# Sinkhorn attention in front of an expert layer: k and v mixed on the chip, straight into the layouts that attention reads

## The chip, the cores and the metric

The kernel runs on one core of one Trainium2 chip. The metric is the device time of one execution in microseconds (us), lower is better. A profile of one execution, with a trace of every instruction and transfer, is there for each kernel. The executions compared here were all in the fast state, apart from two small measuring kernels with a single run each, whose state is unknown. Some of them came from other chips of the same kind, on which the kernel before took 717 to 719 us instead of 710, so kernels from different chips are compared by their ratio to the kernel before, timed in the same rounds on the same chip.

Engine names in the profile: PE is TensorE (PEld its weight loads), DVE is VectorE, ACT is ScalarE, POOL is GpSimd, SP is SyncE, which here only issues transfers.

## The reference

Attention with sorted blocks, then a layer with eight experts. The change concerns the first part alone.

```python
B, H, S, D = 4, 8, 768, 64          # 32 heads; 8 blocks of 96 rows each
P = sort_net                        # [4, 8, 8, 8]
for _ in range(5):                  # Sinkhorn
    P = exp(P - P.max(-1)); P = P / P.sum(-1); P = P / P.sum(-2)
k_sorted = einsum('bhij,bhjcd->bhicd', P, k_b)   # block i is a mix of 8 blocks
v_sorted = einsum('bhij,bhjcd->bhicd', P, v_b)
attn = softmax(q_b @ k_sorted^T / sqrt(D))       # inside each block of 96 rows
x = attn @ v_sorted                 # to [3072, 512], row = (batch, position)
# then: router picks one of 8 experts a row (argmax of x @ w_gate + bias);
# out[row] = gate * relu(x[row] @ w1[e]) @ w2[e]
```

## The kernel before

P is normalised on VectorE, written to memory and read back as block-diagonal 128x128 matrices `bd`, with 32 small loads. Sixteen heads at a time, one matmul mixes 512 columns of k or v; the result goes to scratch memory. Attention then reads q, mixed k and mixed v head by head in runs of one 64-element row.

```python
for g in range(2):
    # ... bd: 16 loads of 8x8 blocks of P from memory ...
    for which, src_v, dst_v in ((0, k_bh, ks_v), (1, v_bh, vs_v)):
        rhs = sb.tile([128, BLK * D], BF16)          # ... loaded ...
        for c in range(12):
            acc = psum.tile([128, 512], FP32)
            nc.tensor.matmul(acc, bd, rhs[:, c * 512:(c + 1) * 512], start=True, stop=True)
            res = sb3.tile([128, 512], BF16)
            nc.scalar.copy(res, acc)                 # dense eviction
            nc.gpsimd.dma_start(out=dst_v[...][:, c * 512:(c + 1) * 512], in_=res)
# ...
for bh in range(BH):
    if bh % 4 == 1: load_weights(bh // 4)            # two loads of 1 MB
    # ... loads of q, mixed k, mixed v of this head, 128-byte runs ...
    for g in range(2):
        # 8 transposes of q and k into tp; copy qkT <- tp on VectorE
        # 4 matmuls sc_p = q k^T; exponential on ScalarE
        # row sums and reciprocal on VectorE
        # 4 transposes of attn into atp; copy attnT <- atp on VectorE
        # 4 matmuls o_p = attnT v
        # 4 scalings by the reciprocal, half on VectorE, half on ScalarE
    # after 8 heads: x rows stored
```

The router, the prefix sums, the scatters of row numbers and the expert loop follow; they are the same in both kernels.

The softmax here doesn't subtract the row's maximum and nothing guards it: scores larger than these inputs give would overflow.

Of the kernel before, what the change touches and what calls it, by code (L numbers as in the profile page):

```python
# [9 lines left out]
FP32 = mybir.dt.float32  # L10
# [7 lines left out]
def kernel(  # L18
# [23 lines left out]
    P_dram = nc.dram_tensor("P_scratch", [BH, NB, NB], FP32, kind="Internal").ap()  # L42
    ks_dram = nc.dram_tensor("ks_scratch", [BH, NB, BLK, D], BF16, kind="Internal").ap()
    vs_dram = nc.dram_tensor("vs_scratch", [BH, NB, BLK, D], BF16, kind="Internal").ap()
# [9 lines left out]
    singles = ctx.enter_context(tc.tile_pool(name="singles", bufs=1))  # L54
    ph1 = ExitStack()
    sb = ph1.enter_context(tc.tile_pool(name="sb", bufs=2))
    sb3 = ph1.enter_context(tc.tile_pool(name="sb3", bufs=3))
    psum = ph1.enter_context(tc.psum_pool(name="psum", bufs=2))
    psum2 = ph1.enter_context(tc.psum_pool(name="psum2", bufs=2))

    ident = singles.tile([128, 128], BF16)
    make_identity(nc, ident)

    P_t = singles.tile([BH, NB, NB], FP32)
    nc.gpsimd.dma_start(out=P_t, in_=sort_net.rearrange("b h i j -> (b h) i j"))
    red = singles.tile([BH, NB], FP32)
    for it in range(5):
        nc.vector.tensor_reduce(red, P_t, AX.X, ALU.max)
        nc.vector.tensor_tensor(P_t, P_t, red.broadcast_to([BH, NB, NB]), ALU.subtract)
        nc.scalar.activation(P_t, P_t, ACT.Exp)  # L70
        nc.vector.tensor_reduce(red, P_t, AX.X, ALU.add)
        nc.vector.reciprocal(red, red)
        nc.vector.tensor_tensor(P_t, P_t, red.broadcast_to([BH, NB, NB]), ALU.mult)
        P_swap = bass.AP(tensor=P_t.tensor, offset=P_t.offset,
                         ap=[P_t.ap[0], P_t.ap[2], P_t.ap[1]])
        nc.vector.tensor_reduce(red, P_swap, AX.X, ALU.add)
        nc.vector.reciprocal(red, red)
        colb = bass.AP(tensor=red.tensor, offset=red.offset,
                       ap=[red.ap[0], [0, NB], red.ap[1]])
        nc.vector.tensor_tensor(P_t, P_t, colb, ALU.mult)  # L80
    nc.gpsimd.dma_start(out=P_dram, in_=P_t)

    k_bh = k.rearrange("b h (n c) d -> (b h) n (c d)", n=NB)
    v_bh = v.rearrange("b h (n c) d -> (b h) n (c d)", n=NB)
    ks_v = ks_dram.rearrange("g n c d -> g n (c d)")
    vs_v = vs_dram.rearrange("g n c d -> g n (c d)")

    for g in range(2):
        bd = sb.tile([128, 128], BF16)
        nc.vector.memset(bd, 0.0)  # L90
        for l in range(16):
            bh = g * 16 + l
            src = bass.AP(tensor=P_dram.tensor, offset=P_dram.offset + bh * 64,
                          ap=[[1, NB], [NB, NB]])
            nc.gpsimd.dma_start(out=bd[l * 8:(l + 1) * 8, l * 8:(l + 1) * 8], in_=src)  # L95
        for which, src_v, dst_v in ((0, k_bh, ks_v), (1, v_bh, vs_v)):
            rhs = sb.tile([128, BLK * D], BF16)
            nc.gpsimd.dma_start(
                out=rhs.rearrange("p (a f) -> p a f", a=16),
                in_=src_v[g * 16:(g + 1) * 16].rearrange("g n f -> (g n) f")  # L100
                    .rearrange("p (a f) -> p a f", a=16))
            for c in range(12):
                acc = psum.tile([128, 512], FP32)
                nc.tensor.matmul(acc, bd, rhs[:, c * 512:(c + 1) * 512],  # L104
                                 start=True, stop=True)
                res = sb3.tile([128, 512], BF16)
                nc.scalar.copy(res, acc)  # L107
                nc.gpsimd.dma_start(  # L108
                    out=dst_v[g * 16:(g + 1) * 16]
                        .rearrange("g n f -> (g n) f")[:, c * 512:(c + 1) * 512],  # L110
                    in_=res)

    ph1.close()
    I32 = mybir.dt.int32
    from concourse.masks import make_upper_triangular
    wpool = ctx.enter_context(tc.tile_pool(name="wpool", bufs=1))
    w1_all = wpool.tile([128, E, 4 * F], BF16, tag="w1_all")
    w2_all = wpool.tile([128, E, 8 * Dm], BF16, tag="w2_all")
# [35 lines left out]
    scale = 1.0 / (D ** 0.5)  # L154
    ph2 = ExitStack()
    apool = ph2.enter_context(tc.tile_pool(name="apool", bufs=3))
    apsum = ph2.enter_context(tc.psum_pool(name="apsum", bufs=2))
    for bh in range(BH):
        b, h = bh // H, bh % H
        if bh % 4 == 1:  # L160
            load_weights(bh // 4)
        if h == 0:
            xacc = [apool.tile([BLK, 4, H, D], BF16, tag=f"xacc{gg}",
                               name=f"xacc{gg}")
                    for gg in range(2)]
        qks = apool.tile([BLK, NB, 2, D], BF16)
        nc.gpsimd.dma_start(out=qks[:, :, 0],  # L167
                            in_=q[b, h].rearrange("(n r) d -> r n d", r=BLK))
        nc.scalar.dma_start(out=qks[:, :, 1],
                            in_=ks_dram[bh].rearrange("n r d -> r n d"))  # L170
        vs_all = apool.tile([BLK, NB, D], BF16)
        nc.sync.dma_start(out=vs_all,
                            in_=vs_dram[bh].rearrange("n r d -> r n d"))
        for g in range(2):
            tp = apsum.tile([D, 8 * BLK], BF16, tag="tp")
            for j in range(4):
                nc.tensor.transpose(tp[:, j * BLK:(j + 1) * BLK],  # L177
                                    qks[:, 4 * g + j, 0], ident[:BLK, :BLK])
                nc.tensor.transpose(tp[:, (4 + j) * BLK:(5 + j) * BLK],  # L179
                                    qks[:, 4 * g + j, 1], ident[:BLK, :BLK])  # L180
            qkT = apool.tile([D, 8 * BLK], BF16, tag="qkT")
            nc.vector.tensor_copy(qkT, tp)  # L182
            sc_p = apsum.tile([BLK, 4 * BLK], FP32, tag="sc")
            for j in range(4):
                nc.tensor.matmul(sc_p[:, j * BLK:(j + 1) * BLK],  # L185
                                 qkT[:, j * BLK:(j + 1) * BLK],
                                 qkT[:, (4 + j) * BLK:(5 + j) * BLK],
                                 start=True, stop=True)
            attn = apool.tile([BLK, 4, BLK], BF16, tag="attn")
            nc.scalar.activation(attn.rearrange("p a f -> p (a f)"), sc_p,  # L190
                                 ACT.Exp, scale=scale)
            rs = apool.tile([BLK, 2, 4], FP32, tag="rs")
            nc.vector.tensor_reduce(rs[:, 0], attn, AX.X, ALU.add)  # L193
            nc.vector.reciprocal(rs[:, 1], rs[:, 0])
            atp = apsum.tile([BLK, 4 * BLK], BF16, tag="atp")
            for j in range(4):
                nc.tensor.transpose(atp[:, j * BLK:(j + 1) * BLK],  # L197
                                    attn[:, j], ident[:BLK, :BLK])
            attnT = apool.tile([BLK, 4 * BLK], BF16, tag="attnT")
            nc.vector.tensor_copy(attnT, atp)  # L200
            o_p = apsum.tile([BLK, 4 * D], FP32, tag="op")
            for j in range(4):
                nc.tensor.matmul(o_p[:, j * D:(j + 1) * D],  # L203
                                 attnT[:, j * BLK:(j + 1) * BLK],
                                 vs_all[:, 4 * g + j], start=True, stop=True)
            for j in range(4):
                if j % 2 == 0:
                    nc.vector.tensor_scalar(xacc[g][:, j, h],  # L208
                                            o_p[:, j * D:(j + 1) * D],
                                            rs[:, 1, j:j + 1], None, ALU.mult)  # L210
                else:
                    nc.scalar.activation(xacc[g][:, j, h],  # L212
                                         o_p[:, j * D:(j + 1) * D],
                                         ACT.Copy, scale=rs[:, 1, j:j + 1])
        if h == H - 1:
            for gg in range(2):
                dst = bass.AP(
                    tensor=x_dram.tensor,
                    offset=x_dram.offset + (b * S + 4 * gg * BLK) * Dm,
                    ap=[[Dm, BLK], [BLK * Dm, 4], [1, H * D]])  # L220
                nc.sync.dma_start(
                    out=dst, in_=xacc[gg].rearrange("p j h d -> p j (h d)"))
# [203 lines left out]
```

## Time and profile before

The kernel took 710.56 us (median of the 3 runs made before the prediction, 709.73 to 712.48). The lines that bear on the argument are shown in the prediction; this table sums up where they put the time.

| Stage of the kernel before | from, to (us) | what sets it |
|---|---|---|
| Sinkhorn, `bd` | 0 to 31 | small VectorE steps, then the loads of `bd` |
| mix of k and v | 31 to 100 | stores of the mixed blocks |
| attention | 100 to 306 | 32 heads at 5.27 us are 169 us; the other 37 us are lost to q loads behind weights |
| router, prefix sums | 306 to 386 | many small steps |
| scatters of row numbers | 386 to 488 | 24 transfers one after the other |
| experts | 488 to 711 | matmuls, gathers of rows |

The 306 us at which attention ends is the moment when its last store of x is issued; that store landed at 309.4 us.

### The profile page before, as it was taken

The page shows a single profiled execution, that of the slowest core. Times are in us where ns is not written, and L with a number is a line of the kernel's source. Part 1 is how long each engine was busy: PE and PEld are TensorE (multiplying, and loading weights), DVE is VectorE, ACT ScalarE, POOL GpSimd, SP SyncE. Part 2 cuts the span into 40 slices and gives each one's busy share as a digit, 9 for nine tenths or more (in the row PEclk, how much of TensorE's full clock was granted, in tenths as well). Part 3 has the DMA queues.
Part 4 walks back from the last instruction along what each step waited for, and adds up shares of the span by engine and source line. Part 5 has one row for each costly group of instructions (what it writes and reads, how often), then busy time and mean ns, then how long its engine had stood idle before and what let it go on. Part 6 is the DMA issues. An engine that isn't in the chain of part 4 may idle for free.

```text
span 711.1 us, 8406 instructions
## 1 busy us (share of the span) xinstructions
PE 368.2 (52%) x2424; PEld 217.2 (31%) x2442; DVE 248.1 (35%) x936; ACT 190.8 (27%) x611; POOL 188.6 (27%) x263
## 2 busy tenths in 40 slices
PE   0133364388665788845520000001887788777782
PEld 0000033376554676623310000000333333333331
DVE  4000014367454667745540000000334344443431
ACT  1033342134232333435530000000333333232331
POOL 3863352032120111002212222222233232232231
PEclk9999999999999999999999999999999999999998
DMA  8567559999999755133300000000121111221110
GB/s 164 46 141 166 142 120 116 180 195 213 191 197 212 80 85 70 17 101 64 61 0 6 0 1 0 0 0 23 38 68 52 60 65 46 68 67 45 41 24 0
DMA packets 117106, 56.27 MB, mean 79 GB/s; under 512 B 93964, under 2 KB 108373, under 8 KB 116550
## 3 DMA queue, kind: packets, MB, share of 16 engines
q0 software_dynamic: 51456, 43.04, 33.7%
q1 hardware_dynamic: 37062, 6.39, 6.9%
q10 hardware_dynamic: 28544, 6.30, 5.3%
q8 instruction: 21, 0.34, 0.2%
q14 instruction: 23, 0.19, 0.1%
HBM read 66.13 MB, written 17.63 MB: 118 GB/s over the span
## 4 chain that ended last, share of the span: by engine, by line
DMA 36%; PE 27%; issue 18%; POOL 7%; DVE 7%; ACT 3%; POOLq 0%; SPq 0%; ACTq 0%; DVEq 0%
DMA qks<-in_q_dram 12%; DMA sidx_scratch<-rg_all,dest_i_all 11%; PE h_p L373 6%; PE y_p L388 5%; DMA x_t<-x_scratch,idxg 4%; PE sc_p L185 3%; PE tp L177 3%; DMA out_dram<-y_sb,idxg 3%; PE hT_p L384 2%; PE atp L197 2%; PE tp L179 2%; DVE y_sb L392 2%; DMA idxg<-sidx_scratch 2%; POOL bd L95 2%; POOL ks_scratch L108 2%
## 5 line engine op out<-in xcount | busy, mean ns | idle before, releaser
L367 PE MATMUL xT_p<-ident,x_t 128*128 128x128 bf16 x124 | 20.5, 221 | 143.5 <-DMA x_t<-x_scratch,idxg 127.7
L388 PE MATMUL y_p<-w_all,hT 128*128 x237 | 72.9, 377 | 0.8 <-ACT hT L385 0.8
L177 PE MATMUL tp<-ident,qks 96*64 96x96 bf16 x256 | 49.1, 283 | 32.4 <-DMA qks<-in_q_dram 30.6
L182 DVE COPY qkT<-tp 64x768 bf16<-64x768 bf16 x64 | 34.6, 540 | 88.4 <-PE tp L179 88.4
L361 POOL DMA_INDIRECT x_t<-x_scratch,idxg x31 | 30.4, 980 | 129.8 <-PE h_p L373 56.9
L373 PE MATMUL h_p<-w_all,xT 128*128 x241 | 59.0, 386 | 10.1 <-issue 8.6
L104 PE MATMUL acc<-rhs,bd 128*128 128x512 bf16 x48 | 27.2, 586 | 71.2 <-ACT res L107 39.2
L167 POOL DMA_DIRECT2D qks<-in_q_dram x32 | 24.9, 779 | 143.9 <-PE tp L179 139.6
L368 ACT COPY xT<-xT_p 128x128 bf16<-128x128 bf16 x62 | 16.4, 265 | 170.1 <-PE xT_p L367 169.8
L212 ACT ACTIVATE xacc<-o_p,rs 96x64 bf16<-96x64 f32 x128 | 39.3, 307 | 73.6 <-DVE xacc L208 72.5
L367 PEld LDWEIGHTS <-x_t 128*128 128x128 bf16 x124 | 9.5, 97 | 150.0 <-DMA x_t<-x_scratch,idxg 133.5
L384 PE MATMUL hT_p<-ident,h_sb 128*128 128x128 bf16 x248 | 49.5, 220 | 10.2 <-DVE hT L385 9.0
L368 DVE COPY xT<-xT_p 128x128 bf16<-128x128 bf16 x62 | 12.2, 219 | 115.2 <-PE xT_p L367 114.8
L177 PEld LDWEIGHTS <-qks 96*64 96x64 bf16 x256 | 37.3, 159 | 39.6 <-DMA qks<-in_q_dram 32.4
L179 PE MATMUL tp<-ident,qks 96*64 96x96 bf16 x256 | 48.6, 281 | 0.0
L190 ACT ACTIVATE attn<-sc_p 96x384 bf16<-96x384 f32 x64 | 31.1, 486 | 65.0 <-PE sc_p L185 63.9
L185 PE MATMUL sc_p<-qkT 64*96 64x96 bf16 x256 | 42.6, 290 | 7.2 <-DVE qkT L182 7.0
L343 POOL DMA_INDIRECT sidx_scratch<-rg_all,dest_i_all x24 | 23.3, 971 | 79.7 <-DMA sidx_scratch<-rg_all,dest_i_all 75.4
L208 DVE TENSOR_SCALAR xacc<-o_p,rs 96x64 bf16<-96x64 f32 x128 | 35.1, 274 | 25.5 <-PE o_p L203 23.7
L385 DVE COPY hT<-hT_p 128x128 bf16<-128x128 bf16 x124 | 27.9, 225 | 45.5 <-PE hT_p L384 39.4
L107 ACT CAST res<-acc 128x512 bf16<-128x512 f32 x48 | 27.4, 586 | 59.7 <-DMA vs_scratch<-res 26.6
L193 DVE TENSOR_REDUCE rs<-attn 96x4 f32<-96x384 bf16 x64 | 35.0, 547 | 21.7 <-ACT attn L190 21.5
(117 smaller groups left out, 659.2 us busy)
## 6 DMA issues: line engine op xcount, KB each, us to landing
w_all<-in_moe_w_dram POOLq DMA_DIRECT2D x16, 1024.0 KB, 13.3
rhs<-in_k_dram POOLq DMA_DIRECT2D x2, 1536.0 KB, 10.9
rhs<-in_v_dram POOLq DMA_DIRECT2D x2, 1536.0 KB
qks<-in_q_dram POOLq DMA_DIRECT2D x32, 96.0 KB, 16.3
ks_scratch<-res POOLq DMA_DIRECT2D x24, 128.0 KB, 2.1
vs_scratch<-res POOLq DMA_DIRECT2D x24, 128.0 KB, 2.0
qks<-ks_scratch ACTq DMA_DIRECT2D x32, 96.0 KB, 8.7
vs_all<-vs_scratch SPq DMA_DIRECT2D x32, 96.0 KB, 9.6
```

Source lines behind the costliest of these rows:

```text
L177: nc.tensor.transpose(tp[:, j * BLK:(j + 1) * BLK], qks[:, 4 * g + j, 0], ident[:BLK, :BLK])
L179: nc.tensor.transpose(tp[:, (4 + j) * BLK:(5 + j) * BLK], qks[:, 4 * g + j, 1], ident[:BLK, :BLK])
L182: nc.vector.tensor_copy(qkT, tp)
L185: nc.tensor.matmul(sc_p[:, j * BLK:(j + 1) * BLK], qkT[:, j * BLK:(j + 1) * BLK], qkT[:, (4 + j) * BLK:(5 + j) * BLK], start=True, stop=True)
L190: nc.scalar.activation(attn.rearrange("p a f -> p (a f)"), sc_p, ACT.Exp, scale=scale)
L193: nc.vector.tensor_reduce(rs[:, 0], attn, AX.X, ALU.add)
L208: nc.vector.tensor_scalar(xacc[g][:, j, h], o_p[:, j * D:(j + 1) * D], rs[:, 1, j:j + 1], None, ALU.mult)
L212: nc.scalar.activation(xacc[g][:, j, h], o_p[:, j * D:(j + 1) * D], ACT.Copy, scale=rs[:, 1, j:j + 1])
L361: nc.gpsimd.indirect_dma_start(out=x_t, out_offset=None, in_=x_dram, in_offset=bass.IndirectOffsetOnAxis(ap=idx[:, :1], axis=0))
L373: nc.tensor.matmul(h_p, xT[:, c], w1_flat[:, bass.ds(e_sv * (4 * F) + c * F + half * 512, 512)], start=(c == 0), stop=(c == 3))
L384: nc.tensor.transpose(hT_p, h_sb[:, fc * 128:(fc + 1) * 128], ident)
L388: nc.tensor.matmul(y_p, hT[:, fc], w2_flat[:, bass.ds(e_sv * (8 * Dm) + fc * Dm, Dm)], start=(fc == 0), stop=(fc == 7))
```

## The change

The intent is to take the scratch memory for P and for mixed k and v out of the kernel. The matrices `bd` are built on chip. The mix is written with the data as the weights and `bd` as the moving operand, so its result comes out already transposed as the scores want it (k: head dimension on partitions) and as the value matmul wants it (v: block row on partitions). The scores are computed transposed (k rows on partitions), so the exponential writes the operand of the value matmul directly, without transposes; a column of ones beside v gives the row sums. q is loaded in runs of six rows (768 bytes). The core of the diff, with cuts:

```diff
-    for bh in range(BH):
-        ... loads of q, ks, vs; transposes; scores; row sums; transposes; values ...
+    def sort_k(g, ch, act):
+        acc = mipsum.tile([128, 8, 64], FP32, tag="mi", name=f"ka{g}_{ch}")
+        for z in range(8):
+            nc.tensor.matmul(acc[:, z], k_il[:, ch * 8 + z].rearrange("p r d -> p (r d)"), bd_k[g], start=True, stop=True)
+        dst = kTb[g].rearrange("p (x c) -> p c x", c=BLK)[:, ch * 8:(ch + 1) * 8]
+        (nc.scalar.copy if act else nc.vector.tensor_copy)(dst, acc)
+
+    def sort_v(g, ch, act):
+        acc = mipsum.tile([128, 4, 128], FP32, tag="mi", name=f"va{g}_{ch}")
+        for z in range(4):
+            nc.tensor.matmul(acc[:, z], v_cols[:, ch * 4 + z], bd_v[g], start=True, stop=True)
+        dst = v_sb[g].rearrange("p x d -> p d x")[0:BLK, ch * 4:(ch + 1) * 4]
+        (nc.scalar.copy if act else nc.vector.tensor_copy)(dst, acc[0:BLK])
...
+    def expo(u):
+        nc.scalar.activation(attnT[u % 3][...], sc_tiles.pop(u)[0:BLK, :, 0:4 * BLK], ACT.Exp, scale=scale)
...
+    def av(u):
+        if h == 0:
+            x_tiles[g, hf] = apool.tile([BLK, 2, 4, H, D], BF16, tag="xb", bufs=1)
+        for par in range(2):
+            ... 4 matmuls of attnT and v with its column of ones ...
+            nc.vector.reciprocal(rs, op[0:BLK, :, D:D + 1])
+            nc.vector.tensor_tensor(xb[:, par, :, h], op[0:BLK, :, 0:D], rs.broadcast_to([BLK, 4, D]), ALU.mult)
+        if h == 7:
+            for par in range(2):
+                for t in range(6):
+                    nc.sync.dma_start(out=dst, in_=xb[t * 16:(t + 1) * 16, par]...)   # 12 stores of 64 KB
...
+    for e in range(3, E):
+        load_weights(e)          # the space of these held q, k and v until here
```

There are 32 units of attention, each half of the blocks of two heads; 16 units make a group, and the 28 "sort jobs" (12 of k, 16 of v) of group 0 come before the first unit, those of group 1 between the units of group 0.

## The prediction

> **What bounds the kernel now.** I cut the span into stages first, because the page's mean shares (PE 52%, DVE 35%) mix stages with different limits. The chain of waits gives the joints: mixing starts when bd has landed (31 us), the first q transpose stands at 100, the last x store at 306, the last count lands at 368, the scatters of row numbers run from 386 to 488, the expert loop from 488.5 to the end. The view by windows, one row a stage (columns: window, length, then PE, PEld, DVE, ACT, POOL busy us with counts, clock, DMA share, GB/s):
>
> ```profile
> 0.00:20.50 20.50, 0.00 (x0) 0.00 (x0) 8.61 (x42) 2.56 (x6) 5.44 (x13) 1.00 0.90 162
> 20.50:100.00 79.50, 27.22 (x48) 4.97 (x48) 0.00 (x0) 27.32 (x48) 44.48 (x81) 1.00 0.56 125
> 100.00:306.00 206.00, 147.27 (x1280) 117.88 (x1280) 120.67 (x390) 67.35 (x193) 37.77 (x52) 1.00 1.03 138
> 306.00:366.00 60.00, 30.57 (x239) 18.66 (x239) 32.97 (x240) 27.97 (x142) 11.72 (x24) 1.00 0.29 65
> 366.00:386.00 20.00, 0.97 (x7) 0.53 (x7) 3.09 (x16) 1.09 (x7) 4.43 (x9) 1.00 0.04 5
> 386.00:488.50 102.50, 0.00 (x0) 0.00 (x0) 0.00 (x0) 0.00 (x0) 22.99 (x24) 1.00 0.01 0
> 488.50:711.00 222.50, 162.14 (x850) 75.15 (x868) 82.77 (x248) 64.51 (x217) 61.74 (x62) 0.99 0.16 48
> ```
>
> The change works on the first three rows, 306 us; the other 405 us (router, prefix sums, scatters, experts) keep their code. In row two TensorE works 27 of 79.5 us: mixed k and v leave through 48 stores, and the next eviction waits for a store to land. In row three the chain of waits shows two regimes. With the weights in flight:
>
> ```profile
> 111.53 30.32 DMA qks<-in_q_dram
> ...
> 174.26 19.14 DMA qks<-in_q_dram
> 196.50 17.76 DMA qks<-in_q_dram
> 217.37 20.02 DMA qks<-in_q_dram
> ```
>
> Four q loads of 96 KB hold everything for 87 us together; they sit behind 1 MB weight loads on the same queue. Once the weights are in, one head starts every 5.27 us:
>
> ```profile
> 242.22 0.55 PE sc_p L185 x4
> 247.49 0.55 PE sc_p L185 x4
> 252.76 0.55 PE sc_p L185 x4
> ```
>
> So attention is 32 x 5.27 = 169 us by compute, plus about 37 us of load stalls. Which engine sets 5.27 us? From the groups view (mean ns at the end of the busy time):
>
> ```profile
> L182 DVE COPY qkT<-tp 64x768 bf16<-64x768 bf16 x64 | 34.6, 540 | 88.4 <-PE tp L179 88.4
> L193 DVE TENSOR_REDUCE rs<-attn 96x4 f32<-96x384 bf16 x64 | 35.0, 547 | 21.7 <-ACT attn L190 21.5
> L200 DVE COPY attnT<-atp 96x384 bf16<-96x384 bf16 x64 | 22.0, 344 | 34.7 <-PE atp L197 34.4
> L208 DVE TENSOR_SCALAR xacc<-o_p,rs 96x64 bf16<-96x64 f32 x128 | 35.1, 274 | 25.5 <-PE o_p L203 23.7
> L190 ACT ACTIVATE attn<-sc_p 96x384 bf16<-96x384 f32 x64 | 31.1, 486 | 65.0 <-PE sc_p L185 63.9
> L107 ACT CAST res<-acc 128x512 bf16<-128x512 f32 x48 | 27.4, 586 | 59.7 <-DMA vs_scratch<-res 26.6
> ```
>
> Per head VectorE does 2 x (0.540 + 0.547 + 0.164 reciprocal + 0.344) + 4 x 0.274 = 4.3 us. TensorE issues 40 matmuls, which follow each other every 0.08 us in the chain (100.41, 100.49, 100.57 ...), so 3.2 us. Both are near the pace, and the hand-overs between engines make the rest: 5.27 / 4.3 = 1.23, a factor that I use below.
>
> [...] the ks and vs loads are 128 B runs, 96 KB in 8.7 and 9.6 us, while 128 KB of x_t in 1 KB runs takes 2.5 us; 93964 of 117106 packets are under 512 B. [...]
>
> **The change part by part.** Removed: the round trip of P and 32 bd loads (15 to 31 us on the chain), 48 stores and 64 short-run loads of mixed k and v, the transposes of k and of the scores with their copies, the row-sum reductions, and the 128 B runs of q (now 768 B).
>
> (a) Start to mixed group 0. Sinkhorn keeps its pace, 14.5 us less a few (only one max and subtraction). It now shares VectorE with two clearing memsets of k_il (a bd memset of 64 words took 0.112; 3072 words are about 2.8 us each, an estimate) and 12 k copies. The block matrices come from two small matmuls and ten short VectorE steps, some 3 us. Loads: 163 GB/s over the first 18 us, really from 2.4 us on, gives 188 GB/s in bytes written; k, v and two q loads are 1.57 + 1.57 + 0.8 MB, 21 us. k arrives in six pieces through two buffers, and in this trace weight loads run well ahead of the source order (the last of the 16 is issued at 211 us, at about head 18, though the source asks for it at head 29). The weights of experts 0 to 2 depend on nothing now, so one to six of them (5.6 us each at 188 GB/s) will slip in front of late k pieces. I take bd ready at 30 to 35 us. Then 28 sort jobs: 8 or 4 matmuls (0.64 or 0.4 us), an eviction of 512 columns (586 ns ACT, 692 ns for DVE's h_sb), two PSUM buffers: (0.6 + 0.25 + 0.65 + 0.2) / 2 = 0.85 us a job, 24 us. With k late, attention begins at about 60 us.
>
> (b) Attention: 32 units, each as much as one old head. TensorE: 8 + 8 matmuls and 3 transposes, 19 x 0.08 = 1.5 us. [...] VectorE: two reciprocals (0.17) and two products of 256 columns [...], and half a qT copy (0.27): 1.5 us. Times 1.23: 1.9 us, taken as 2.0. Units 0 to 15 carry 28 sort jobs as well: 14 evictions, 12 k copies, q interleaves add some 18 us of VectorE, so (1.5 + 1.1) x 1.23 = 3.2 us a unit. Sum: 16 x 3.2 + 16 x 2.0 = 83 us.
>
> (c) New waits. The x buffer is single and leaves in 12 stores of 64 KB on one issuing engine: 12 x 0.3 to 0.5 us (the old x store's issue) + 2 to 3 us landing = 7 us, at three joints and at the end: 4 x 6 = 24 us over what is hidden, little of it hidden. k and q of group 1 behind weights on the same ring, with a copy at the head of VectorE's order: 5 us.
>
> Sum: 60 + 83 + 24 + 5 = 172 us in place of 306, saving 134.
>
> (d) Weights give some back. q, kT and the inputs now lie in the space of experts 3 to 7, so these ten 1 MB loads can't start before those regions are dead. Parts of 4 to 7 are dead after group 1 is mixed; both loads of expert 3, w2 of 4 and w1 of 5 wait for the last scores. Four loads x 5.6 = 22 us, and the router's count stores stand behind them on the ring; cnt_sb has three buffers, so the router does three tiles (about 10 us) and stalls until they land: about 10 us lost. If all ten come at the end it is 56 - 10 = 46 us.
>
> 710.6 - 134 + 10 = 587 us.
>
> **Rivals.** First, the weights become the new wait in full (46 us in place of 10): for it, the 30 us stall behind weights and that the source places these loads after attention; against it, weights run ahead of source order in this trace. 620 us. Second, VectorE's order is fixed with optimistic arrivals, and late k copies block Sinkhorn and evictions: attention begins at 85 us, group 0 runs at 4.5 us a unit; 630 us. For it: one engine, in order, and six pieces through two buffers. Third, evictions into strided columns (2-byte elements 192 or 130 bytes apart) and strided v weights cost double: 56 evictions x 0.6 over two engines is 17 us, plus 128 weight loads x 0.1 = 13 us; 610 us. No row of the trace has such a write. Fourth, all hides well: attention begins at 45, units at 1.8 and 2.6 us, stores hidden, no weight stall: 45 + 70 + 10 + 405 = 530 to 545 us. Fifth, nothing gained because TensorE or the loads bound the stage anyway: the 87 us of q stalls and 52 of 79 idle us on TensorE speak against it.
>
> **Range and chances.** Rivals one to three each add 25 to 45 us and can add up partly; the fourth takes off 45. Hence 587 us, 550 to 632 with 8 in 10. To lose 2% more than 134 us would have to be given back; even rivals one to three together come to about 690. Faster 0.97, same 0.02, slower 0.01.
>
> **What would show it.** Right: no DMA wait on scratch k and v; the first score matmul at 50 to 75 us; the last products at 155 to 190 us; scores of units 18 to 30 spaced about 2 us; VectorE the busiest engine in attention; a gap in the router three tiles in, ended by a count store; scatters and experts unchanged within 2 us. Wrong: attention longer than 120 us with TensorE waiting on VectorE (rival two or three, told apart by the mean of the strided evictions, 0.65 or over 1 us), a router stage of over 85 us (rival one), or under 62 us (no weight stall), or an expert loop that moves.

## The result, and the profile after

The changed kernel took 627.24 us (median of 4 runs, 625.43 to 628.88); the kernel before, on the same chip, 710.23 us. The ratio is 0.8831 (95% interval 0.8799 to 0.8864). Ratios are the mean time of one kernel's runs over that of the other's in the same rounds, so not quite the ratio of the medians. So 83 us were saved where the prediction's sum had 123: inside its range, 5 us below the upper end.

The windows view of the changed kernel by its own stages (window, length, then PE, PEld, DVE, ACT and POOL busy us with counts, clock, DMA share, GB/s):

```profile
0.00:50.20 50.20, 1.10 (x18) 1.04 (x19) 22.18 (x69) 2.56 (x6) 16.72 (x35) 1.00 0.99 132
50.20:97.00 46.80, 13.98 (x151) 11.85 (x149) 40.55 (x27) 35.65 (x14) 5.45 (x9) 1.00 0.81 133
97.00:157.00 60.00, 34.14 (x400) 27.32 (x399) 49.26 (x65) 44.21 (x27) 10.63 (x14) 1.00 0.77 133
157.00:207.00 50.00, 26.47 (x302) 18.22 (x300) 23.89 (x77) 13.31 (x17) 0.90 (x1) 1.00 0.57 95
207.00:231.00 24.00, 6.31 (x70) 3.96 (x68) 7.99 (x29) 3.23 (x4) 2.54 (x4) 1.00 0.90 161
231.00:288.00 57.00, 30.39 (x241) 18.78 (x241) 33.40 (x242) 28.62 (x145) 11.67 (x24) 1.00 0.26 58
...
405.00:626.00 221.00, 163.91 (x850) 76.31 (x868) 81.98 (x248) 64.71 (x217) 61.89 (x62) 0.99 0.16 48
```

The last store of x landed at 230.1 us, in place of 309.4. Of the 84.8 us between the two traced executions (711.1 and 626.3 us), 79 lie before that moment and 5 to 6 after it, in unchanged code. In the second row, the mix of group 0, VectorE is busy 41 of 47 us with only 27 instructions, and ScalarE 36 us with 14: few, long instructions. In the third row they are busy 49 and 44 of 60 us, while attention of group 0 runs beside the mix of group 1. The last two rows belong to code that did not change (router 57 us, experts 221; before 60 and 222.5).

What the long instructions are, from the groups (mean ns after the busy time, then idle time before them and its cause):

```profile
L175 DVE CAST v_sb<-va 96x512 bf16<-96x512 f32 x16 | 39.1, 2445 | 10.2 <-PE va L173 10.1
L175 ACT CAST v_sb<-va 96x512 bf16<-96x512 f32 x16 | 39.3, 2454 | 12.5 <-PE va L173 12.5
L168 DVE CAST w_all<-ka 128x512 bf16<-128x512 f32 x12 | 32.5, 2710 | 1.9 <-PE ka L166 1.8
L236 DVE TENSOR_TENSOR xb<-op,rs 96x256 bf16<-96x256 f32 x64 | 26.0, 417 | 18.5 <-DMA x_scratch<-xb 16.9
```

The evictions of the mix take 2.45 us (v) and 2.71 us (k); with ScalarE's dozen for k (2712 ns each) they are 56 instructions and 143 us of two engines. The dense eviction of 512 columns before took 0.586 us. The last line carries a second finding: VectorE stood idle 16.9 us until stores of x had read the single buffer.

The chain of waits (start us, us, what) shows the same in order of time, with two more things, a wait for k at the start and four long waits for x stores:

```profile
24.73 15.69 DMA k_raw<-in_k_dram
...
53.43 2.73 DVE w_all L168
...
194.49 6.56 DMA x_scratch<-xb
201.06 5.07 DMA x_scratch<-xb
...
216.77 7.13 DMA x_scratch<-xb
223.92 6.20 DMA x_scratch<-xb
```

Why the mix began at 50 us only, VectorE's timeline shows (start us, us, instruction, in brackets the idle time before it and what ended it):

```profile
18.14 0.63 DVE L99 COPY q_il<-q_in 128x768 bf16<-128x768 bf16 x2 [8.45 <-DMA q_in<-in_q_dram]
...
27.78 0.25 DVE L127 TENSOR_REDUCE red<-P_t 32x8 f32<-32x64 f32 x1
40.45 0.86 DVE L71 COPY w_all<-k_raw 64x1024 bf16<-64x1024 bf16 x2 [12.42 <-DMA k_raw<-in_k_dram]
41.34 0.19 DVE L128 RECIPROCAL red<-red 32x8 f32<-32x8 f32 x1
```

Lines 127 and 128 are two successive steps of one Sinkhorn iteration. A copy of a piece of k was put between them in VectorE's order, and that piece came 12.42 us later. The reciprocal had nothing to wait for but its place behind the copy. The first line shows the same thing earlier: Sinkhorn's first step on VectorE came at 21.93 us, behind a copy of q for which the engine had stood 8.45 us.

### The profile page after: what moved, and what is told of

It is laid out like the page before. It is cut to its first block, busy times and chain, and to the rows that moved or that the text cites. A ratio compares the mean times of both kernels' runs of the same rounds, so it can differ in the third digit from the quotient of the medians.

```text
span 626.3 us, 6878 instructions
## 1 busy us (share of the span) xinstructions
PE 277.0 (44%) x2026; PEld 157.8 (25%) x2044; DVE 261.8 (42%) x769; ACT 192.7 (31%) x431; POOL 137.3 (22%) x180
## 4 chain that ended last, share of the span: by engine, by line
DMA 29%; PE 27%; issue 16%; DVE 15%; ACT 8%; POOL 3%; SPq 1%; POOLq 0%; DVEq 0%; ACTq 0%
DMA sidx_scratch<-rg_all,dest_i_all 12%; PE h_p L462 8%; PE y_p L477 7%; DMA x_scratch<-xb 4%; PE hT_p L473 3%; ACT v_sb L175 3%; DVE v_sb L175 3%; DVE y_sb L481 3%; DMA x_t<-x_scratch,idxg 3%; DVE w_all L168 3%; DMA k_raw<-in_k_dram 3%; DMA q_in<-in_q_dram 2%; ACT w_all L168 2%; DMA out_dram<-y_sb,idxg 2%; PE va L173 2%
## 5 line engine op out<-in xcount | busy, mean ns | idle before, releaser
L175 DVE CAST v_sb<-va 96x512 bf16<-96x512 f32 x16 | 39.1, 2445 | 10.2 <-PE va L173 10.1
L175 ACT CAST v_sb<-va 96x512 bf16<-96x512 f32 x16 | 39.3, 2454 | 12.5 <-PE va L173 12.5
L474 ACT COPY hT<-hT_p 128x128 bf16<-128x128 bf16 x124 | 32.8, 264 | 29.8 <-PE hT_p L473 26.1
L219 ACT ACTIVATE attnT<-sc 96x768 bf16<-96x768 f32 x32 | 26.8, 841 | 48.9 <-PE op L232 39.1
L482 POOL DMA_INDIRECT out_dram<-y_sb,idxg x31 | 31.4, 1014 | 25.9 <-DVE xT L457 13.2
L462 PEld LDWEIGHTS <-xT 128*128 128x128 bf16 x248 | 24.7, 99 | 46.3 <-issue 25.7
L168 ACT CAST w_all<-ka 128x512 bf16<-128x512 f32 x12 | 32.5, 2712 | 8.3 <-PE ka L166 8.3
L477 PEld LDWEIGHTS <-hT 128*128 128x128 bf16 x248 | 23.9, 96 | 44.0 <-issue 16.5
L481 DVE TENSOR_SCALAR y_sb<-y_p,idxg 128x512 f32<-128x512 f32 x31 | 23.3, 751 | 27.3 <-PE y_p L477 26.4
L236 DVE TENSOR_TENSOR xb<-op,rs 96x256 bf16<-96x256 f32 x64 | 26.0, 417 | 18.5 <-DMA x_scratch<-xb 16.9
```

The costliest lines, as they stand in the source:

```text
L168: (nc.scalar.copy if act else nc.vector.tensor_copy)(dst, acc)
L175: (nc.scalar.copy if act else nc.vector.tensor_copy)(dst, acc[0:BLK])
L219: nc.scalar.activation(attnT[u % 3][:, 0:8 * BLK].rearrange("p (r f) -> p r f", r=2), sc_tiles.pop(u)[0:BLK, :, 0:4 * BLK], ACT.Exp, scale ...
L462: nc.tensor.matmul(h_p, xT[:, c], w_all[:, bass.ds(e_sv * WCOL + c * F + half * 512, 512)], start=(c == 0), stop=(c == 3))
L474: (nc.scalar.copy if fc % 2 else nc.vector.tensor_copy)(hT[:, fc], hT_p)
L477: nc.tensor.matmul(y_p, hT[:, fc], w_all[:, bass.ds(e_sv * WCOL + 4 * F + fc * Dm, Dm)], start=(fc == 0), stop=(fc == 7))
```

## The experiments

**The theories.** A: the evictions are slow because of how they write: single 2-byte elements far apart (192 bytes for k, 130 for v). B: they are slow because two engines evict at once. C: they are slow because of the order in which PSUM is read. Beside them, three smaller terms: late k copies in VectorE's order, the single x buffer, and the number of stores. A fourth question is why the router did not stall for the weights.

In each row below, "against the changed kernel" is the difference of the two ratios to the kernel before, times its 717 us on these chips. The last column is read in the trace: when the last store of x landed, 230.1 us in the changed kernel. It is the cleaner figure for this stage, though it comes from one trace a kernel, because what follows it, with unchanged code, took 395 to 407 us in these traces (401 in the kernel before), apart from the late-weights run. The profiled executions of five of these kernels had a mean granted clock (the share of its full speed at which TensorE was allowed to run) of 0.73 to 0.76, the others of 0.987 or more; that part doesn't follow it (401.5 us at 0.989 and 401.6 at 0.733 in the last two). The interval of one ratio is 2 to 4 us wide on either side, so a difference of 3 us is not clear of noise.

| Kernel | median us | ratio to before (95%) | against the changed kernel, us | last x store landed |
|---|---|---|---|---|
| changed | 627.24 | 0.8831 (0.8799 to 0.8864) | | 230.1 |
| dense evictions (wrong values) | 584.0 | 0.8147 (0.8114 to 0.8181) | -49 | 186.5 |
| evictions in runs | 592.62 | 0.8282 (0.8241 to 0.8324) | -39 | 186.4 |
| two x buffers | 609.95 | 0.8523 (0.8463 to 0.8583) | -22 | 202.2 |
| Sinkhorn ahead of the copies | 630.94 | 0.8793 (0.8749 to 0.8837) | -3 | 224.8 |
| the same, group 1's copies later | 617.15 | 0.8595 (0.8565 to 0.8625) | -17 | 215.1 |
| two stores in place of twelve | 627.05 | 0.8727 (0.8695 to 0.8759) | -7 | 222.3 |
| weights all at the end | 662.96 | 0.9236 (0.9201 to 0.9271) | +29 | 222.6 |
| best, two stores | 579.22 | 0.8064 (0.8037 to 0.8091) | -55 | 179.0 |
| best, twelve stores | 584.16 | 0.8123 (0.8092 to 0.8154) | -51 | 182.1 |

### The eviction measured by itself, twice

The first measuring kernel holds nothing but copies of 512 columns from PSUM, written in different patterns, on VectorE alone, on ScalarE alone, and on both at once. Its output is zeros.

```python
for name, d, s in forms(dv, sv):         # dense, step 2..96, runs of 2, 4, 8, strided read
    for r in range(3): nc.vector.tensor_copy(d, s)
# ... the same on ScalarE, then both engines side by side:
nc.vector.tensor_copy(dv2.rearrange("p (x c) -> p c x", c=96)[:, 0:8], sv2)
nc.scalar.copy(av2.rearrange("p (x c) -> p c x", c=96)[:, 0:8], sa2)
```

> A kernel of copies alone (its result is zeros on purpose): 512 elements a partition from PSUM float32 to bf16, dense, with steps of 2, 4, 8, 12 and 96 elements, in runs of 2, 4 and 8, and read with a step but written densely; on VectorE alone, ScalarE alone, then both at once; also a float32 output with the same 192-byte step and an SBUF source. Theory A (the scattered two-byte writes cost): dense 0.6 to 0.7 us, step 96 about 2.7 us on either engine alone, a float32 output cheaper or equal, runs of 8 near 0.7 to 1 us, the strided read with a dense write near 0.7 us. Rival B (the two engines slow each other): alone under 1 us, both at once 2.5 us. Rival C (the PSUM read order or the source costs): the dense write with a strided read is slow as well, and the SBUF source is fast.

All forms had one source line, and the profile merged them into one group (a mean of 1243 ns over eleven forms), so the question of the pattern stayed open. The two engines side by side gave 2716 ns (VectorE) and 2717 ns (ScalarE) for the far step. The second measuring kernel repeats it with one line of source a form.

> The copies of the first form test once more, each form with a row of its own in the profile (the first test showed step 96 at 2.7 us on both engines at once, but merged the rest). Theory A (each separate two-byte place costs about 4.9 ns once places are far apart): dense 0.6 to 0.7 us, step 2 and 4 cheaper than step 96, step 96 2.7 us on each engine alone, runs of 8 as dense, strided read with dense write as dense. Rival C (read order costs): the strided read is slow. The float32 output tells whether two-byte width or distance is what costs: near 1 to 1.2 us if width.

The groups of VectorE (line, form, mean ns):

```profile
L43 DVE CAST v_step<-psv 128x512 bf16<-128x512 f32 x3 | 8.4, 2787 | 0.1
L37 DVE CAST v_step<-psv 128x512 bf16<-128x512 f32 x3 | 7.3, 2432 | 0.1
L61 DVE COPY v_sbsrc<-sbs 128x512 bf16<-128x512 bf16 x3 | 4.3, 1426 | 0.0
L34 DVE CAST v_step<-psv 128x512 bf16<-128x512 f32 x3 | 3.9, 1283 | 0.1
L58 DVE COPY v_f<-psv 128x512 f32<-128x512 f32 x3 | 3.5, 1183 | 0.0
L31 DVE CAST v_step<-psv 128x512 bf16<-128x512 f32 x3 | 2.2, 723 | 0.1
L52 DVE CAST v_run<-psv 128x512 bf16<-128x512 f32 x3 | 2.1, 687 | 0.1
L28 DVE CAST v_dense<-psv 128x512 bf16<-128x512 f32 x3 | 2.0, 670 | 0.1
```

From the bottom: dense (L28) 670 ns; runs of 8 elements (L52) 687; one element in 2 (L31) 723; one in 4 (L34) 1283; one in 8 (L37) 2432; one in 96, the step of the kernel's k (L43), 2787. Runs of 4 took 688, runs of 2 774. Reading PSUM with a stride and writing densely took 688 ns, so theory C falls. VectorE alone is as slow as both engines together (2787 and 2716), so theory B falls; ScalarE alone shows the same row, 586 dense, 1291 for one in 4, 2454 for one in 8, 2829 for one in 96. Theory A stands: the cost is in the write pattern, it more than quadruples the copy (670 to 2787 ns on VectorE, 586 to 2829 on ScalarE), and runs of four elements avoid it (688 ns). Two lines complicate the picture: the same step with 4-byte elements (L58) took 1183 ns, and 2-byte elements from an SBUF source (L61) 1426. By the sign set in advance ("near 1 to 1.2 us if width") the first says that the width of two bytes counts. But the second also writes two bytes, and takes half as long. So the far single 2-byte write out of fp32 in PSUM is dearest; no run here shows why these two are cheaper.

### Dense evictions, wrong values

Everything as in the changed kernel, but the same 512 elements are written side by side. The values land in the wrong places. A clearing of the part of `v_sb` that then stays unwritten is added.

```diff
-        dst = kTb[g].rearrange("p (x c) -> p c x", c=BLK)[:, ch * 8:(ch + 1) * 8]
+        dst = kTb[g][:, ch * 512:(ch + 1) * 512]            # and v alike
```

> The changed kernel with the 56 evictions of the mix written densely, in the wrong order (the result is wrong on purpose). Theory A (scattered writes set the mix stage): evictions fall from 2.45 and 2.71 us to 0.6 to 0.7 us, the first mix from 47 to about 25 us, group 1's share of the first 16 units shrinks too (60 to about 45 us); in all 30 to 40 us off the changed kernel's 627, so 587 to 597. Rival (TensorE or the two PSUM buffers set the mix stage): under 10 us off.

The evictions fell to 685 ns (VectorE) and 583 ns (ScalarE) for v, 683 and 580 for k, and the last x store landed at 186.5 us, 43.6 us earlier. That is the whole price of the pattern on the path, more than the 30 to 40 us expected: the mix of group 0 took 28 us in place of 47, and the rest came in the units of group 0 beside the other mix. By engine time it is (143.4 - 35.5) / 2 = 54 us for an even split. Not all of that came through: the chain now shows waits for loads in the mix and after it (10.86 us for a piece of k from 51 us on, 13.35 us for q from 102 us on).

### Evictions in runs, right values

The elements go to the same places as in the changed kernel, but the two loops of the copy are exchanged: the inner one now runs over neighbouring addresses, 8 for k and 4 for v, and the stride falls on the read side.

```diff
-        dst = kTb[g].rearrange("p (x c) -> p c x", c=BLK)[:, ch * 8:(ch + 1) * 8]
-        (nc.scalar.copy if act else nc.vector.tensor_copy)(dst, acc)
+        dst = kTb[g].rearrange("p (x c) -> p x c", c=BLK)[:, :, ch * 8:(ch + 1) * 8]
+        (nc.scalar.copy if act else nc.vector.tensor_copy)(dst, acc.rearrange("p c x -> p x c"))
# v: v_sb[g][0:BLK, :, ch * 4:(ch + 1) * 4] <- acc[0:BLK].rearrange("p d x -> p x d")
```

> The changed kernel with the same destinations, but the loops of each eviction exchanged, so that it writes runs of 8 elements (k) and 4 (v) and reads PSUM with a step; the result stays right. Theory A (cost per scattered write, shared by the elements of a run): evictions of 0.7 to 1.2 us, 20 to 35 us off 627. Rival (cost per element of a strided output or of PSUM order): evictions stay at 2 us or more, within 5 us of 627.

```profile
L175 DVE CAST v_sb<-va 96x512 bf16<-96x512 f32 x16 | 12.8, 797 | 7.6 <-PE va L173 7.4
L168 DVE CAST w_all<-ka 128x512 bf16<-128x512 f32 x12 | 8.2, 683 | 1.4 <-PE ka L166 1.3
```

From 2445 to 797 ns and from 2710 to 683 ns, with the output correct. The last x store landed at 186.4 us, as in the dense kernel: the reordering of two loops recovers all of it. Both the 39 us by ratio and the 44 us of path are more than the 20 to 35 us expected. Of the 10 us by which the ratios of the two experiments differ, 6 lie after that store in the traces, in the unchanged part (395.4 and 401.4 us); the rest stays open.

### Two x buffers

```diff
-            ... tag="xb", name=f"xb{g}_{hf}", bufs=1)
+            ... tag="xb", name=f"xb{g}_{hf}", bufs=2)
```

> The changed kernel with two x buffers in place of one. Theory (the 12 stores at each joint hold the next product): the waits of 6 and 11 us before products in the second half go, 15 to 20 us off 627, and the 14 us of stores at the end stay. Rival (the wait is hidden elsewhere or the stores just pile up on their queue): under 5 us.

```profile
L236 DVE TENSOR_TENSOR xb<-op,rs 96x256 bf16<-96x256 f32 x64 | 25.0, 413 | 1.2 <-DVE rs L235 0.2
```

The 16.9 us of waits for stores in front of this line are gone. The last x store landed 28 us earlier, more than the waits and more than the 15 to 20 us expected. The rest may be order: in the changed kernel no exponential runs between 134 and 165 us, while the sort jobs of v run alone; with two buffers six exponentials begin in that stretch. The likely reason, which no run isolates, is that the order of the instructions was laid out with the wait for the single buffer in it. The pair of stores at the end stayed (6.12 and 5.60 us on the chain).

### Sinkhorn ahead of the copies

The Sinkhorn steps are placed ahead of the copies of k and q for group 0 in VectorE's order, and k gets six raw buffers instead of two, so that its loads do not depend on the copies.

```diff
+    # Sinkhorn moved up, its last product named p_last
-    load_k(0)
-    load_v(0)
+    with tc.issue_after(p_last.ins):       # these instructions are ordered behind it
+        load_k(0)
+        load_v(0)
# the same around load_q(0, 0) and load_q(0, 1); k_raw bufs=2 -> 6
```

> The changed kernel with VectorE's order mended: Sinkhorn is issued ahead of all copies of k and q, and six k buffers let all six k loads go at once; evictions stay scattered. Theory (the late copies in front of Sinkhorn cost the start): block matrices ready at 25 to 30 us in place of 49, and the whole ends 15 to 22 us earlier than 627. Rival (the loads themselves bound the start, whatever the order): under 6 us.

`bd` was ready at 32 us instead of 49, as the prediction had it (this run's own expectation was 25 to 30), but only some 5 us came of it on the path, and 3 by ratio. By the number alone that is the rival. But Sinkhorn itself ended at 18 us. Then two waits for q (1.70 and 5.30 us), again before copies, held the last steps to `bd`, and the timeline of VectorE shows the 12 us wait of before in another place:

```profile
46.99 0.96 DVE L71 COPY w_all<-k_raw 64x1024 bf16<-64x1024 bf16 x2 [11.08 <-DMA k_raw<-in_k_dram]
```

This copy belongs to group 1. It now stands ahead of the evictions of group 0, which had all they needed.

### The same, with group 1's copies behind the mix of group 0

```diff
-            load_k(1)
+            with tc.issue_after(mixed0.ins):    # the last VectorE eviction of group 0
+                load_k(1)
```

> The run with Sinkhorn first and six k buffers, and in addition VectorE's copies of group 1's k queued behind the last eviction of group 0 (evictions still scattered). In the Sinkhorn-first run the block matrices were ready at 32 us, but VectorE then stood 11 us (36 to 47) before a copy of group 1's k whose load lay behind weights: the wait had moved, not gone. If that wait is all, the first mix ends near 33 + 46 = 79 us in place of 91, and the whole comes to 612 to 620 where the changed kernel has 627. Rival (q or k of group 1 then stops the first units instead): the first mix ends early, but the end moves by less than 4 us from the Sinkhorn-first run.

The mix of group 0 now ran from 33.3 to 77.9 us, and the last x store landed at 215.1 us, 15 us before that of the changed kernel and 10 us before that of the last experiment. By ratio the gain over the changed kernel is 17 us. So the fixed order was worth about 15 us, in two places at once; to undo one only moved the wait to the other. (The waits for q before `bd` are still there.)

### Two stores in place of twelve

The columns of transposed q are put in natural order, so that a buffer of x leaves in one store a batch.

```diff
-        qT = w_all[...].rearrange("p (i t r) -> p i t r", i=NB, t=6)
+        qT = w_all[...].rearrange("p (i r t) -> p i r t", i=NB, t=6)
-                for t in range(6): nc.sync.dma_start(...)        # 64 KB each
+                nc.sync.dma_start(out=dst, in_=xb[:, par].rearrange("p i h d -> p i (h d)"))
```

> The changed kernel with q's columns put in natural row order while they are copied out of PSUM, so that x leaves in 2 stores of 96 partitions at each joint in place of 12 of 16 partitions. Theory (the many stores from 16 partitions each are slow in themselves): the waits of 6 and 11 us in the second half shrink to 3 or 4, the last stores take 4 in place of 14 us; 15 to 25 us off 627. Rival (the weight loads that share the DMA engines slow the stores): the last stores still take 10 us or more, and under 10 us are won.

The gain was 7 us, and the last stores still took over 10 us: what the rival had said. The wait at 174 us (at one of the joints, where a full x buffer must be stored before the next unit can write it) went from 8 to 4 us, but the later ones stayed long: in the chain, 10.47 us from 189.53 and 12.21 us from 210.07. Where they are long, the number of stores is not the main reason. At these two, weight loads had just been issued (at 188.30, and from 203.61 to 206.15 us); before the joint at 174 us the last ones were issued at 161 us.

### All weights of experts 3 to 7 at the very end

In the changed kernel these ten loads go out as their space comes free. Here they are all placed behind the last value product, to see the mechanism by which the prediction gave 10 us back.

```diff
+    last = nc.gpsimd.memset(attnT[31 % 3][:, 8 * BLK:], 0.0)   # waits for the last products
+    with tc.issue_after(last.ins):
+        for e in range(3, E): load_weights(e)
```

> The changed kernel with all ten weight loads of experts 3 to 7 issued after the last product (a memset that has to wait for it stands in front of them). My prediction's step on weights (ten loads of 5.6 us stand in front of the router's counts on one ring): the router stalls three or four tiles in until the weights have landed, the scatters begin 25 to 45 us later than in the changed kernel, 650 to 672 us. Rival (the counts don't wait for the weights, or the router hides them): within 8 us of 627.

```profile
197.78 2.06 DMA x_scratch<-xb
...
233.48 37.27 DMA cnt_scratch<-cnt_sb
```

The second line is the predicted stall in full: a small store of counts waited 37.27 us behind the weight loads. So the store did stand behind the loads, as (d) of the prediction had it, and it cost 29 us in the total. The first line is a by-product. At the joint in the middle of group 1, where no weights are in flight here, the last store landed 2.06 us after some 6 us in which the twelve were issued; in the changed kernel, which has a weight load in flight at that point, the chain shows 6.56 and 5.07 us of store waits there. Twelve stores have to be issued in both, so the gain is smaller than these pieces: VectorE's waits for stores came to 12.0 us in all, in place of 16.9. So some 5 us of the store waits are the price of weight loads that go out earlier.

### A version that beats both

Runs, Sinkhorn first, six raw k buffers, late copies of group 1, two stores, and the weights of experts 0 to 2 ordered behind the loads of group 1's k. The second x buffer was left out for want of space, which no run shows.

```diff
+            with tc.issue_after(k1_dma.ins):
                 load_weights(WLOAD[u])
```

> All mended together: Sinkhorn first with six k buffers, group 1's copies behind the first mix, evictions in runs, one store per batch at each joint, and the weights of experts 0 to 2 issued behind group 1's k. If the found costs add up: start 17, evictions 40, group 1's copies 11, stores some 7: 627 - 70 = 557, give or take 12. If group 0's mix and attention become bound by loads (k, v, q, weights on one ring), 575 to 590.

It took 579.22 us and was correct: 0.8064 of the kernel before, 0.913 of the changed one as the quotient of the two ratios. The costs did not add up to 557 us; the time lies in the rival's range. The chain says why it is no faster:

```profile
56.00 30.51 DMA q_in<-in_q_dram
...
167.18 11.78 DMA x_scratch<-xb
```

With the mix down to 19 us (33.3 to 52.5), q of later heads is late by 30.51 us. Ahead of it on the queue stood five weight loads, issued from 37.53 to 45.37 us, and v of group 1. That wait has the same form as the 30.32 us in the kernel before. The bound has gone from VectorE back to the loads.

The same kernel with the twelve stores of the changed one:

> As the run with everything mended, but with the 12 stores of 16 partitions at each joint. With the stores as a cost of their own: 5 to 12 us longer than that run; if it is the weight loads that slow the stores, within 4 us.

It took 584.16 us, 4 us slower by ratio and 3 us later at the last x store: at the border between the two expectations. Alone, the two stores gave 7 us by ratio and 8 on the path. With the noise of the ratios, these runs don't tell 4 from 7. The 3 us are seen at the end: from the first issue of the last stores to the landing, 11.78 us with two and 14.4 with twelve. VectorE's waits for stores in between were not shorter with two (21.5 and 17.0 us).

## Why the prediction was right, and what was off

The direction, what would go and the range were right: the scratch round trips went, no wait for scratch k or v is left, and the router, scatters and experts keep their times within 5 us (57 for 60, 98 for 102.5, 221 for 222.5). The size was off by 40 us of the 123 that the sum had as saving. Term by term:

| Term of the sum | predicted us | measured us |
|---|---|---|
| (a) `bd` ready | 30 to 35 | 49 |
| (a) 28 sort jobs of group 0 | 24 | 47 |
| (b) units 0 to 15 with the mix of group 1, and (c) group 1's loads | 51 + 5 | 77 |
| (b) units 16 to 31 | 32 | 25 |
| (c) waits for stores at the joints | 18 | 17 |
| (c) stores at the end | 6 | 14 |
| sum to the last x store | 172 | 230 |
| (d) router's stall | 10 | 0 |

So the stage that was changed took 58 us longer than the sum. The whole missed by only 40, because the router's stall did not come (10 us) and the rest took 396 us where the sum allowed 405. That these two went the other way is luck.

**The mis-sized term.** The step that failed is "an eviction of 512 columns (586 ns ACT, 692 ns for DVE's h_sb)". Both durations come from rows that write densely; the new ones write single elements 192 and 130 bytes apart and took 2.45 to 2.71 us. The third rival saw the place but sized it as "cost double", 17 us over two engines; it was a factor of about four, and the dense and the run kernels measure it at 44 us of the path. That is as much as the second and third lines of the table are over together (23 and 21 us), though part of the third line yields to a second x buffer as well. Its other half, strided weight loads of v at 0.1 us more each, shows as 183 ns a load against 128 for k; no run took it by itself. (Its two terms, 17 and 13 us, also add up to 617, not 610.) The prediction said itself that no row of the trace has such a write.

**`bd` at 49 us.** This is the second rival in part: "late k copies block Sinkhorn and evictions". It was right on the mechanism, a 12.42 us wait in the middle of a Sinkhorn iteration, and its size was about 15 us, as the two reordering experiments show. Rivals one to three were held to be able to "add up partly", and two of them did. The second rival's own figures (attention from 85 us, 4.5 us a unit, 630 us) come close to the measured 98, 4.8 and 627. But most of that was the work of the evictions, so the agreement is luck. (The two clearing memsets took 2.62 us each, where the prediction's estimate was 2.8.)

**Attention's pace.** Without the mix, a unit took 1.6 us, not 2.0:

```profile
169.72 0.82 ACT attnT L219
171.41 0.82 ACT attnT L219
```

The prediction's 1.5 us of VectorE a unit leaves about 0.45 us for each of the two products. That was the estimate, which no row of the trace before shows; the product took 417 ns. The exponential took 0.82 us here (841 ns in the mean of all 32). VectorE's work in these units was less than the 1.5 us. The copies of q for group 1 had all been made before 165 us, which leaves 8.91 us for 31 instructions from 182.5 to 194.2 us, 1.15 us a unit in place of 1.5. The pace is 1.4 times that, so the run does not show that the factor of 1.23 for hand-overs was too much. Nor was this part of attention a matter of VectorE alone: the chain goes from the exponential to scores and value products and back, and TensorE is busy 9.11 of these 11.7 us. Up to 165 us, beside the mix, VectorE was the busiest engine (55 of 68 us, ScalarE 45).

**The stores.** Waits at the joints came out as summed (6.03 and 10.85 us), those at the end twice as long. The late-weights run shows what the estimate lacked: beside a weight load the stores landed late (6.56 and 5.07 us on the chain at the joint in group 1, 2.06 us without), and that made up about 5 of the 10.85 us. At the end weight loads are in flight in both kernels, and there the stores took as long in the late-weights run too (6.53 and 5.58 us).

**The router's stall.** The mechanism exists, 37.27 us in the late-weights run. It was hidden in the changed kernel: most loads went out earlier, the last three were issued at 210 to 212 us, and the first count was stored at 237 us only, after the stores of x and the first tiles of the router. By then nothing stood before it.

**Signs named in advance.** The first score matmul at 50 to 75 us: wrong, 98. The last products at 155 to 190 us: wrong, 216. The mean of the evictions was named as the way to tell rival three: at 2.45 us and more it pointed to it at once. The gap in the router: not there; its stage of 57 us is the sign "under 62 us (no weight stall)". Scores about 2 us apart: 1.6. VectorE the busiest engine in attention: only beside the mix. Scatters and experts within 2 us: the experts were, the scatters were 4 us shorter. Attention longer than 120 us, the sign of rival two or three: it was, from 97 us to the landing of x at 230.

**Readings that do not hold.** The prediction takes the four q loads to "hold everything for 87 us together". They are the lengths of pieces of the chain, and the engines worked during them: in the 19.14 us from 174.26 ScalarE carried out 17 instructions and VectorE 34. What was lost is the 37 us that it names a little later. It also sets the 8.7 and 9.6 us of the ks and vs loads, in 128-byte runs, against the 2.5 us of x_t in runs of 1 KB. From 242 us on, with the weights in, the ks loads landed in 2.2 us and the vs loads in 2.4 (medians; 9.7 and 10.5 between 100 and 242 us), about as fast as x_t. So this trace does not show that the short runs were what made them slow; the same loads were slow only while weights were in flight beside them.

What stays open: why an SBUF source and 4-byte elements pay less for the same step (1426 and 1183 ns where the 2-byte write from PSUM took 2787); whether two x buffers on top of the best version would pay; and why the unchanged part of the kernel took 395 to 407 us in different traces.

## What to carry to other kernels

When a result leaves PSUM in a new layout, let the inner loop of the eviction write at least four neighbouring elements and put the stride on the read side; the same 512 elements then took 0.7 to 0.8 us instead of 2.4 to 2.8. A copy placed ahead of other steps on VectorE held them until its load had come: 12.42 us in front of a reciprocal that had its data, and, with Sinkhorn moved ahead, 11.08 us in front of evictions that had theirs. So after such a wait is removed, look in the timeline for the next place where it turns up. Once the bound is gone, read the chain again: here the waits for q behind the weights, which the change had removed from the top of the list, came back as the next bound (30.51 us).
